# Queries of an attention block: transposed on TensorE, or loaded in 128-byte runs and turned on VectorE

## The chip, the cores and the metric

The kernel runs on one core of a Trainium2 chip. The metric is the time of one execution on the device in microseconds (us); shorter is better. TensorE multiplies matrices, VectorE and ScalarE work on elements, GpSimd reduces over partitions here, and SyncE (SP) issues all DMAs, in the order in which they are written.

## The reference

Attention over pooled keys and values, then a feed-forward layer with squared Relu. There are 8 batches of 576 tokens and 8 heads of 64; keys and values are averaged over groups of 8 tokens, so every token attends to 72 of them.

```python
k_p = k.reshape(B, H, Sp, pool, D).mean(axis=3)
v_p = v.reshape(B, H, Sp, pool, D).mean(axis=3)
scores = scale * np.matmul(q, k_p.transpose(0, 1, 3, 2))
scores = scores - np.max(scores, axis=-1, keepdims=True)
attn = np.exp(scores)
attn = attn / (np.sum(attn, axis=-1, keepdims=True) + 1e-09)
out = np.matmul(attn, v_p)                     # q, k, v: (8, 8, 576, 64) float32
x = out.transpose(0, 2, 1, 3).reshape(B * S, H * D)      # 4608 x 512
h = np.maximum(x @ w_in, 0.0)                  # w_in 512 x 2048
return h * h @ w_out                           # w_out 2048 x 512
```

## The kernel before

The 4608 tokens are cut into 12 chunks of 384 (`CH`). A chunk lies in one batch, or spans two (chunks 1, 4, 7 and 10); `segments` gives its parts. One step is one chunk and one block of 128 hidden columns, 16 steps a chunk. In step s the loop at the end (L691) issues `hidden` of step s on TensorE (12 products of 128x384: high and low parts of x and of the weights, three products for each of four blocks), then the TensorE parts of the attention work that is due in the step, `weigh_values` last, and then `project` of step s - 2 (nine products of 128x512). After them come the parts for the other engines, written in this order: the split of the hidden block of step s - 1 (`split_hidden`: gh on ScalarE, gl on VectorE), what follows the attention's matmuls (the functions that `transpose_q`, `scores` and `weigh_values` return), the stages that issue nothing on TensorE, the conversion of weights, the collected loads, and last Relu and square of step s (ScalarE, VectorE). Every engine keeps the order in which its instructions are written (`InOrder`).

Attention runs ahead of its chunk, one pair of heads after the other, four steps apart (`STEADY`: the first step of each pair, and the offset of each stage from it). A pair's query load is issued `QL` = 4 steps ahead of its first step (`load_q`: 96 partitions, runs of 1 KB or 512 bytes). Then follow `transpose_q` (offset 0: four transposes of 96x128 into PSUM; ScalarE copies the rows of each head from there as the high part, and VectorE subtracts it for the low part, which goes to the other 64 rows, so that a tile st has 128 rows with high and low part stacked), `scores` (1), `exponents` (3: VectorE subtracts the maximum, ScalarE makes exponents, GpSimd sums over the partitions into tot), `send_sums` (4), `fetch_sums` (5), `reciprocals` (6), `fetch_reciprocals` (7) and `weigh_values` (8: av on TensorE; VectorE multiplies by the fetched reciprocals into rb, ScalarE and VectorE split it into xh and xl). Stages 4 to 7 send a row through DRAM with small DMAs.

Tiles that matter here: q lies in a buffer that loads of keys and values share (`LD` = 4); st has one buffer (`STB`). Chunks 0 and 1 are handled in another way: in full precision, with tokens on the partitions.

Loads of keys and values and their pooling (`kv_steps`, VectorE's reductions kp and vp) are spread over the steps before a batch is needed.

Of the kernel before, what the change touches and what calls it, by code (L numbers as in the profile page):

```python
# [9 lines left out]
F32 = mybir.dt.float32  # L10
F32R = mybir.dt.float32r
# [3 lines left out]
ALU = mybir.AluOpType  # L15
# [22 lines left out]
def pooled_attn_relu2_ffn(  # L38
# [16 lines left out]
    PE, DVE, ACT, GP, SP = (InOrder(tc, e) for e in (nc.tensor, nc.vector, nc.scalar, nc.gpsimd, nc.sync))  # L55
    B, H, S, D = q.shape
# [3 lines left out]
    P = 128  # L60
    POOL = 8
    SP_ = S // POOL
# [3 lines left out]
    CH = 384  # L66
    QT = 96
# [4 lines left out]
    KR = KH * SP_  # L72
    KT = KR // QT
    SCALE = 1.0 / (D ** 0.5) / POOL
    LAG, QL = 2, 4

    IDLE = (10, 3)
    STB, SCB, LD, OB = 1, 2, 4, 3
# [5 lines left out]
    SPLIT = 6  # L84


    STEADY = ((-22, -18, -14, -10), (0, 1, 3, 4, 5, 6, 7, 8))
    KV0 = -35
    EARLY = ((-16, -13, -10, -7), (0, 1, 2, 3, 5))

# [6 lines left out]
    sb = ctx.enter_context(tc.tile_pool(name="sb", bufs=2))  # L97
# [21 lines left out]
    def load(dst, src):  # L119
        loads.append((dst, src))  # L120
# [14 lines left out]
    def w_tile(dt, name):  # L135
        return wts.tile([P, 2, 512], dt, name=name, tag="w", bufs=2 * NFC + 1)

    halves = {}

    def half_tile(kind, name):  # L140

        if kind not in halves:
            halves[kind] = w_tile(F32, name)
            return halves[kind][:, 0, :]
        return halves.pop(kind)[:, 1, :]
# [35 lines left out]
    kv, kf, loaded = {}, {}, {}  # L181
# [9 lines left out]
    def ld_tile(shape, name, early):  # L191

        if early:
            return half_tile("l", name)[:shape[0], :shape[1]]
        return sb.tile(shape, F32, name=name, tag="ld", bufs=LD)
# [93 lines left out]
    def segments(c):  # L289
        t, segs = c * CH, []  # L290
        while t < (c + 1) * CH:
            b = t // S
            n = min((b + 1) * S, (c + 1) * CH) - t
            segs.append((b, t - c * CH, n))
            t += n
        return segs

    def load_q(c, p):

        qt = loaded["q", c, p] = ld_tile([QT, 2 * CH // QT * D], f"q_{c}_{p}", c == 0).rearrange("s (h n) -> s h n", h=2)  # L300
        for b, o, n in segments(c):
            s0, g = c * CH + o - b * S, n // QT
            load(qt[:, :, o // QT * D:(o // QT + g) * D],
                 q[b, 2 * p:2 * p + 2, s0:s0 + n, :].rearrange("h (s g) d -> s h (g d)", g=g))

    xts = {}
    live = {}

    def transpose_q(c, p):


        pt = ps_a.tile([P, 512], F32, name=f"qps_{c}_{p}", tag="a")
        blocks = pt[:, :CH].rearrange("p (i t s) -> p i t s", i=2, s=QT)
        qt = loaded.pop(("q", c, p))
        for i in range(2):
            for t in range(NQ // 2):
                PE.transpose(blocks[:, i, t, :], qt[:, i, t * 2 * D:(t + 1) * 2 * D], ident[:QT, :QT])

        def then():
            if c < 2:  # L320
                st = live[c, p] = half_tile("s", f"st_{c}_{p}")[:, :CH]
                ACT.copy(st, pt[:, :CH])
                return
            st = live[c, p] = sb.tile([P, 2, CH], F32R, name=f"st_{c}_{p}", tag="st", bufs=STB)
            order = "p i (s t two) -> p i t s two" if len(segments(c)) == 1 else "p i (t s two) -> p i t s two"
            cols = st.rearrange(order, two=2, s=QT)
            halves = [(slice(i * D, (i + 1) * D), slice((1 - i) * D, (2 - i) * D), i) for i in range(2)]
            for own, oth, i in halves:
                ACT.copy(cols[own, :, :, :, i], blocks[own])
            for own, oth, i in halves:  # L330
                DVE.tensor_tensor(cols[oth, :, :, :, i], blocks[own], cols[own, :, :, :, i].bitcast(F32), op=ALU.subtract)

        return then

    def scores(c, p):

        st = live.pop((c, p))
        ss = [ps_a.tile([P, 512], F32, name=f"sps_{c}_{p}_{i}", tag="a") for i in range(2)]
        for i in range(2):
            h = 2 * p + i  # L340
            for b, o, n in segments(c):
                kh, kl, _ = kv[b]
                for j, kk in enumerate((kl, kh)):
                    PE.matmul(ss[i][:SP_, o:o + n], lhsT=kk[:, h * SP_:(h + 1) * SP_], rhs=st[:, i, o:o + n], start=j == 0, stop=j == 1)

        def then():
            sc = sb.tile([SP_, 2, CH], F32, name=f"sc_{c}_{p}", tag="sc", bufs=SCB)
            mx = reduced("mx", c, p)
            for i in range(2):
                ACT.copy(sc[:, i, :], ss[i][:SP_, :CH])  # L350
                GP.partition_all_reduce(mx[i], sc[:, i, :], channels=SP_, reduce_op=bass_isa.ReduceOp.max)
            live[c, p] = (sc, mx)

        return then

    def reduced(kind, c, p):
        return [sb.tile([SP_, CH], F32, name=f"{kind}_{c}_{p}_{i}", tag="mx", bufs=3) for i in range(2)]
# [210 lines left out]
    for i in range(NKT):  # L568
        load_k(0, i)
        if i % KT == KT - 1:  # L570
            load_q(0, i // KT)
    for p in range(2, NPAIR):
        load_q(0, p)
    for p in range(NPAIR):
        load_v_pair(0, p)
    for i in range(NKT):
        load_k(1, i)
    load_q(1, 0)

    need = {}  # L580
# [14 lines left out]
    for i in range(KT + 2):  # L595
        pool_k(0, i)
    transpose_k(0, 0)()
    transpose_q(0, 0)()
    transpose_q(0, 1)()
    pool_k(0, KT + 2)  # L600
    keep_busy(IDLE[1])
# [4 lines left out]
    for f in reversed(after):  # L606
        f()
    after = [pool_v_pair(0, 2), pool_v_pair(0, 3)]
    transpose_q(0, 2)()
    transpose_q(0, 3)()  # L610
    for f in after:
# [33 lines left out]
    t = 1e9  # L645
    for key in reversed(keys):
        t = min(t - 1 / RATE, need[key] - 1 - MARGIN)
# [22 lines left out]
            at(s + v_at[h] + 2, pool_v, b, h)  # L670

    ready = {0, 1}
    stages = (transpose_q, scores, exponents, send_sums, fetch_sums, reciprocals, fetch_reciprocals, weigh_values)
    for c in range(1, NCH):
        first, offsets = EARLY if c == 1 else STEADY
        names = (transpose_q, token_scores, token_normalise, token_turn, weigh_values) if c == 1 else stages
# [4 lines left out]
        for p in range(NPAIR):  # L681
            s = c * NFC + first[p]
# [5 lines left out]

    last = (to_float32, split_weights)
    on_pe = (transpose_k, transpose_q, scores, token_scores, token_turn, weigh_values)  # L690
    for s in range(-PRO, len(steps) + LAG):  # L691
        todo = work.get(s, [])
# [50 lines left out]
```

## Time and profile before

| | us |
|---|---|
| median of 3 runs | 961.65 (961.38 to 963.41) |
| the profiled execution: its span, first to last instruction | 959.9 |
| TensorE busy (matmuls) | 945.7, 99% |
| VectorE busy | 615.3, 64% |
| ScalarE busy | 451.5, 47% |
| GpSimd busy | 353.7, 37% |
| DMA: 51651 packets, 63.65 MB | 21% of 16 engines for the kernel's own queue |

The execution that the profiler took is described by its span alone; the time of a run also holds what lies around the span, 1.75 us against the median. Busy time of TensorE counts a matmul from its start to its modelled end, so neighbours overlap: what a matmul costs the queue is the distance from its start to the next one's. In a timeline, a number in brackets behind a row is idle time of the engine just before it and what ended it.

### The profile page before, as it was taken

The numbers are of one execution on the slowest core, as the hardware profiler recorded it, in microseconds if no ns is written. First come the engines' busy times: TensorE is split into PE (matmuls) and PEld (weight loads), VectorE is DVE, ScalarE is ACT, GpSimd is POOL, SyncE is SP. The second block draws the span as 40 slices with busy tenths as digits, with TensorE's granted clock in tenths as the row PEclk, the third lists the DMA queues.
The fourth block names the chain that finished last, engine by engine and source line by source line (L and its number), as shares of the span: only waits on it lengthen the run. The fifth ranks groups of instructions, "written<-read, shape, count | busy, mean of one in ns | idle before, by whom it ended". The sixth has DMA issues, their size and how long they took to land.

```text
span 959.9 us, 13537 instructions
## 1 busy us (share of the span) xinstructions
PE 945.7 (99%) x4972; PEld 805.7 (84%) x4972; DVE 615.3 (64%) x1028; ACT 451.5 (47%) x909; POOL 353.7 (37%) x215
## 2 busy tenths in 40 slices
PE   7899999999999999999999999999999999999998
PEld 6657678888888888888888888888888888888997
DVE  7989876667765556677865656766776565553221
ACT  3888766754434344444344344444444444432322
POOL 3900343534344343444353443434443434430000
PEclk9999999999999999999999999999999999999999
DMA  9973111022112112112112012112211210100000
GB/s 271 305 278 96 42 54 64 30 68 80 53 30 77 32 34 68 47 52 88 51 46 72 30 35 83 34 33 78 80 40 43 66 30 18 59 9 9 33 1 34
DMA packets 51651, 63.65 MB, mean 66 GB/s; under 512 B 13936, under 2 KB 32192, under 8 KB 51584
## 3 DMA queue, kind: packets, MB, share of 16 engines
q1 hardware_dynamic: 51584, 62.78, 21.0%
q8 instruction: 39, 0.64, 0.3%
q14 instruction: 28, 0.23, 0.1%
HBM read 53.08 MB, written 9.68 MB: 65 GB/s over the span
## 4 chain that ended last, share of the span: by engine, by line
PE 93%; DMA 4%; DVE 1%; ACT 1%; SPq 1%; issue 0%; DVEq 0%; ACTq 0%
PE o L34 43%; PE h L34 41%; PE av L34 4%; PE sps L34 3%; DMA q<-in_q_dram 2%; PE qps L34 1%; DMA v<-in_v_dram 1%; DMA k<-in_k_dram 1%; DVE wf_o L34 1%; DMA raw_o<-in_moe_w_out_dram 1%; SPq L34 1%; ACT te L34 0%; PE kps L34 0%; PE pps L34 0%; DVE tm L34 0%
## 5 line engine op out<-in xcount | busy, mean ns | idle before, releaser
L34 PE MATMUL h<-xh,w_i 128*128 128x384 f32 x1488 | 417.0, 341 | 0.0
L34 PE MATMUL o<-w_o,gh 128*128 128x512 f32 x1056 | 334.8, 398 | 0.0
L34 PEld LDWEIGHTS h<-xh,w_i 128*128 128x128 f32 x1488 | 272.8, 188 | 10.6 <-issue 2.2
L34 POOL PARTITION_ALL_REDUCE tot<-sc x80 | 201.5, 2566 | 205.9 <-issue 199.5
L34 PE MATMUL h<-xl,w_i 128*128 128x384 f32 x744 | 249.9, 336 | 0.0
L34 PEld LDWEIGHTS o<-w_o,gh 128*128 128x128 f32 x1056 | 192.5, 188 | 51.9 <-issue 16.5
L34 POOL PARTITION_ALL_REDUCE mx<-sc x80 | 119.5, 1541 | 284.6 <-ACT sc L34 284.6
L34 DVE TENSOR_TENSOR gl<-r,gh 128x384 fp32r<-128x384 f32 x176 | 143.5, 816 | 109.1 <-ACT gh L34 108.9
L34 PE MATMUL o<-w_o,gl 128*128 128x512 f32 x528 | 209.1, 396 | 0.0
L34 DVE TENSOR_TENSOR r<-r 128x384 f32<-128x384 f32 x160 | 105.6, 660 | 109.3 <-ACT r L34 108.9
L34 ACT CAST gh<-r 128x384 fp32r<-128x384 f32 x176 | 90.4, 514 | 149.7 <-DVE r L34 149.2
L34 PEld LDWEIGHTS h<-xl,w_i 128*128 128x128 f32 x744 | 139.7, 188 | 10.6 <-issue 3.1
L34 ACT ACTIVATE r<-h 128x384 f32<-128x384 f32 x192 | 94.2, 491 | 101.4 <-PE h L34 100.0
L34 PEld LDWEIGHTS o<-w_o,gl 128*128 128x128 f32 x528 | 99.1, 188 | 22.1
L34 DVE TENSOR_TENSOR st<-qps,st 64x384 fp32r<-64x384 f32 x80 | 60.7, 759 | 61.2 <-ACT st L34 60.3
L34 ACT CAST st<-qps 64x384 fp32r<-64x384 f32 x80 | 59.6, 745 | 58.9 <-PE qps L34 58.4
L34 ACT CAST xh<-rb 128x384 fp32r<-128x384 f32 x40 | 20.5, 513 | 94.6 <-DVE rb L34 94.6
L34 ACT ACTIVATE sc<-sc 72x384 f32<-72x384 f32 x80 | 39.7, 525 | 45.7 <-DVE sc L34 45.7
L34 DVE TENSOR_REDUCE vp<-v 72x64 f32<-72x512 f32 x48 | 50.9, 1061 | 0.0
L34 PE MATMUL av<-sc,vp 72*64 72x384 f32 (+1 forms) x256 | 43.6, 426 | 2.5 <-ACT sc L34 2.5
L34 PE MATMUL o<-wf_o,r 128*128 128x512 f32 x96 | 44.6, 600 | 0.0
L34 DVE TENSOR_REDUCE kp<-k 96x64 f32<-96x512 f32 x42 | 43.9, 1044 | 0.4 <-DMA k<-in_k_dram 0.2
(82 smaller groups left out, 708.7 us busy)
## 6 DMA issues: line engine op xcount, KB each, us to landing
k<-in_k_dram SPq DMA_DIRECT2D x48, 192.0 KB
out_dram<-ob SPq DMA_DIRECT2D x36, 256.0 KB
raw_i<-in_moe_w_in_dram SPq DMA_DIRECT2D x16, 512.0 KB
raw_o<-in_moe_w_out_dram SPq DMA_DIRECT2D x16, 512.0 KB
v<-in_v_dram SPq DMA_DIRECT2D x56, 144.0 KB
rb<-rd SPq DMA_DIRECT2D x80, 96.0 KB
q<-in_q_dram SPq DMA_DIRECT2D x30, 192.0 KB
q<-in_q_dram SPq DMA_DIRECT2D x32, 96.0 KB
```

The costliest lines, as they stand in the source:

```text
L34: return lambda *a, **k: self.tc.keep_in_program_order(f(*a, **k))
```

## The change

Chunks 0 and 1 stay as they are. From chunk 2 on a pair's queries are loaded in other pieces: a tile of 128 partitions by 384, and for each head and each half of its 64 columns one DMA which puts 32 tokens on 32 partitions, with 32 numbers of each, 128 bytes, side by side for every block of 32 tokens. `turn_q` turns the 32x32 blocks on VectorE, so that columns of the head lie on the partitions and tokens along the row, in their order. `split_q` makes the tile st from the turned tile, with the same two copies on ScalarE and two subtractions on VectorE. The matmuls of `scores` are the same, in another order. The loads are issued five steps ahead of the pair's first step, for chunk 1 too; the turn comes one step ahead of it, the split at offset 0. All later stages keep their steps.

```diff
-    LAG, QL = 2, 4
+    LAG, QL = 2, 5
-    STEADY = ((-22, -18, -14, -10), (0, 1, 3, 4, 5, 6, 7, 8))
+    STEADY = ((-22, -18, -14, -10), (-1, 0, 1, 3, 4, 5, 6, 7, 8))
     def load_q(c, p):
+        if c > 1:
+            qt = loaded["q", c, p] = ld_tile([P, CH], f"q_{c}_{p}", False)
+            for b, o, n in segments(c):
+                s0 = c * CH + o - b * S
+                for i in range(2):
+                    for half in range(2):
+                        r = i * D + half * 32
+                        load(qt[r:r + 32, o:o + n].rearrange("j (n e) -> j n e", e=32),
+                             q[b, 2 * p + i, s0:s0 + n, half * 32:half * 32 + 32].rearrange("(n j) e -> j n e", j=32))
+            return
...
         def then():                            # transpose_q
-            if c < 2:
-                st = live[c, p] = half_tile("s", f"st_{c}_{p}")[:, :CH]
-                ACT.copy(st, pt[:, :CH])
-                return
-            st = live[c, p] = sb.tile([P, 2, CH], F32R, name=f"st_{c}_{p}", tag="st", bufs=STB)
-            order = "p i (s t two) -> p i t s two" if len(segments(c)) == 1 else "p i (t s two) -> p i t s two"
-            cols = st.rearrange(order, two=2, s=QT)
-            halves = [(slice(i * D, (i + 1) * D), slice((1 - i) * D, (2 - i) * D), i) for i in range(2)]
-            for own, oth, i in halves:
-                ACT.copy(cols[own, :, :, :, i], blocks[own])
-            for own, oth, i in halves:
-                DVE.tensor_tensor(cols[oth, :, :, :, i], blocks[own], cols[own, :, :, :, i].bitcast(F32), op=ALU.subtract)
+            st = live[c, p] = half_tile("s", f"st_{c}_{p}")[:, :CH]
+            ACT.copy(st, pt[:, :CH])
...
+    def turn_q(c, p):
+        qt = loaded.pop(("q", c, p))
+        live[c, p] = sb.tile([P, CH], F32, name=f"qt_{c}_{p}", tag="qt", bufs=1)
+        DVE.transpose(live[c, p], qt)
+    def split_q(c, p):
+        qt = live[c, p]
+        st = live[c, p] = sb.tile([P, 2, CH], F32R, name=f"st_{c}_{p}", tag="st", bufs=STB)
+        halves = [(slice(i * D, (i + 1) * D), slice((1 - i) * D, (2 - i) * D), i) for i in range(2)]
+        for own, oth, i in halves:
+            ACT.copy(st[own, i, :], qt[own, :])
+        for own, oth, i in halves:
+            DVE.tensor_tensor(st[oth, i, :], qt[own, :], st[own, i, :].bitcast(F32), op=ALU.subtract)
...
     def scores(c, p):
-        for i in range(2):
-            h = 2 * p + i
-            for b, o, n in segments(c):
-                kh, kl, _ = kv[b]
+        for b, o, n in segments(c):
+            kh, kl, _ = kv[b]
+            for i in range(2):
+                h = 2 * p + i
                 for j, kk in enumerate((kl, kh)):
...
-    stages = (transpose_q, scores, exponents, send_sums, fetch_sums, reciprocals, fetch_reciprocals, weigh_values)
+    stages = (turn_q, split_q, scores, exponents, send_sums, fetch_sums, reciprocals, fetch_reciprocals, weigh_values)
```

## Rows read from the trace of the kernel before

**Rows 1.** The page: TensorE's busy time, and its granted clock in 40 slices.
```profile
PE 945.7 (99%) x4972; PEld 805.7 (84%) x4972; DVE 615.3 (64%) x1028; ACT 451.5 (47%) x909; POOL 353.7 (37%) x215
PEclk9999999999999999999999999999999999999999
```
**Rows 2.** The page: the chain that ended last, share of the span by engine.
```profile
PE 93%; DMA 4%; DVE 1%; ACT 1%; SPq 1%; issue 0%; DVEq 0%; ACTq 0%
```
**Rows 3.** Timeline of TensorE, 539.0 to 545: start, us, engine, operation, tiles, shape, count.
```profile
539.33 0.50 PE L34 MATMUL qps<-ident,q 96*128 96x96 f32 x4
539.75 0.87 PE L34 MATMUL av<-sc,vp 72*64 72x192 f32 x8
...
544.85 0.25 PE L34 MATMUL sps<-st,kl 128*72 128x192 f32 x1
```
**Rows 4.** Groups by shape, whole run: form, count, busy us, mean ns, idle before.
```profile
L34 DVE STREAM_TRANSPOSE ramp<-ramp 128x32 f32<-128x32 f32 x1 | 0.2, 211 | 0.0
...
L34 DVE TENSOR_SCALAR ramp<-ramp 128x1 f32<-128x1 f32 x1 | 0.2, 155 | 0.0
```
**Rows 5.** Timeline of VectorE, 532 to 551.
```profile
533.35 1.02 DVE L34 TENSOR_TENSOR sc<-sc,mx 72x384 f32<-72x384 f32 x2
535.92 0.77 DVE L34 TENSOR_TENSOR r<-r 128x384 f32<-128x384 f32 x1 [1.55 <-ACT r L34]
537.27 1.92 DVE L34 TENSOR_TENSOR gl<-r,gh 128x384 fp32r<-128x384 f32 x1 [0.58 <-ACT gh L34]
...
542.06 0.56 DVE L34 TENSOR_TENSOR rb<-av,rb 128x384 f32<-128x384 f32 x1
543.20 0.56 DVE L34 TENSOR_TENSOR xl<-rb,xh 128x384 fp32r<-128x384 f32 x1 [0.58 <-ACT xh L34]
...
549.58 0.16 DVE L34 TENSOR_SCALAR rr<-rc 96x8 f32<-96x8 f32 x1
```
**Rows 6.** Groups by shape in 325 to 400 (chunk 5, one batch).
```profile
L34 ACT CAST st<-qps 64x384 fp32r<-64x384 f32 x8 | 6.8, 851 | 7.7 <-PE qps L34 7.7
L34 DVE TENSOR_TENSOR st<-qps,st 64x384 fp32r<-64x384 f32 x8 | 6.8, 844 | 7.6 <-ACT st L34 7.6
```
**Rows 7.** Groups by shape in 250 to 325 (chunk 4, two batches).
```profile
L34 DVE TENSOR_TENSOR st<-qps,st 64x384 fp32r<-64x384 f32 x8 | 4.4, 556 | 5.2 <-ACT st L34 5.1
L34 ACT CAST st<-qps 64x384 fp32r<-64x384 f32 x8 | 4.0, 501 | 6.7 <-PE qps L34 6.7
```
**Rows 8.** Timeline of GpSimd, 534 to 541.
```profile
534.61 5.01 POOL L34 PARTITION_ALL_REDUCE tot<-sc  x2 [4.57 <-issue]
```
**Rows 9.** Timeline of VectorE, 481.5 to 490: the late pair.
```profile
483.58 1.92 DVE L34 TENSOR_TENSOR gl<-r,gh 128x384 fp32r<-128x384 f32 x1 [0.58 <-ACT gh L34]
```
**Rows 10.** Timeline of TensorE, 481.5 to 489.3: the late pair.
```profile
482.87 0.49 PE L34 MATMUL qps<-ident,q 96*128 96x96 f32 x4
483.30 0.87 PE L34 MATMUL av<-sc,vp 72*64 72x384 f32 x4
...
488.39 0.25 PE L34 MATMUL sps<-st,kl 128*72 128x192 f32 x1
```
**Rows 11.** The tile q: issues on SyncE, duration in ns min/median/max, first and last start.
```profile
L34 SPq DMA_DIRECT2D q<-in_q_dram x62: 325/346/810, 4.5 to 823.1; - x62
```
**Rows 12.** What SyncE's queue waited for: us in total, times, longest.
```profile
SPq L34 <- POOL tot L34: 200.4, 69, 22.0
```
**Rows 13.** DMA in 531.0 to 532.6: queue, packets, MB, share of 16 engines.
```profile
q1 hardware_dynamic: 112, 0.00, 3.6%
```
**Rows 14.** DMA in 521.4 to 524.
```profile
q1 hardware_dynamic: 580, 0.34, 48.6%
```
**Rows 15.** Timeline of SyncE's queue, 538 to 541.
```profile
540.80 0.32 SPq L34 DMA_DIRECT2D rc<-rs  x1
```
**Rows 16.** Timeline of TensorE, 102.4 to 112.5: waits at the start of chunk 2.
```profile
104.35 0.37 PE L34 MATMUL sps<-st,kl 128*72 128x384 f32 x1 [0.83 <-DVE st L34]
...
111.43 0.97 PE L34 MATMUL pps<-ident,te 96*72 96x96 f32 x8 [0.51 <-DVE te L34]
```

More of the change, by code (lines that the diff above doesn't have):

```diff
@@ L338, in scores @@
         ss = [ps_a.tile([P, 512], F32, name=f"sps_{c}_{p}_{i}", tag="a") for i in range(2)]
-        for i in range(2):
-            h = 2 * p + i
-            for b, o, n in segments(c):
-                kh, kl, _ = kv[b]
+        for b, o, n in segments(c):
+            kh, kl, _ = kv[b]
+            for i in range(2):
+                h = 2 * p + i
                 for j, kk in enumerate((kl, kh)):
-                    PE.matmul(ss[i][:SP_, o:o + n], lhsT=kk[:, h * SP_:(h + 1) * SP_], rhs=st[:, i, o:o + n], start=j == 0, stop=j == 1)
+                    PE.matmul(ss[i][:SP_, o:o + n], lhsT=kk[:, h * SP_:(h + 1) * SP_], rhs=st[:, i, o:o + n],
+                              start=j == 0, stop=j == 1)
         def then():
```

## The prediction

> **What bounds the kernel now.** I read the page first: matmuls fill 99% of the span, and the granted clock stays in its top tenth from end to end, so the clock is not where a change can act [rows 1]. The chain that ended last says the same from the other side: 93% of the end time hangs on TensorE's own work, one product behind the next, and the other engines hold it only near the start and the end [rows 2]. Then the timeline of TensorE for one pair of heads in the middle. The reader should look at starts, not at durations, since matmuls overlap: the four query transposes start at 539.33, the weighing of values behind them at 539.75, and nothing stands between [rows 3]. So whatever leaves TensorE's queue shortens the program by its start-to-start time, as long as the operands of the next products are there in time. The rest of the reading is about that condition.
>
> **What is removed.** From chunk 2 on (10 chunks of 4 pairs, 40 pairs), `transpose_q` no longer issues its four transposes: 160 matmuls go. One group of four costs 539.75 - 539.33 = 0.42 us of TensorE's queue, not four times a matmul's own duration; the late pair further on shows 0.43; I take 0.425. 40 x 0.425 = **17.0 us**. The products of `scores` keep their number and sizes; in chunks that span two batches only their order changes, which I cost at nothing. The bank of PSUM that the transposes used is freed.
>
> **What is added on VectorE.** `turn_q`, one transpose of 128x384 per pair, is nowhere in the trace at that size. Nearest rows: the 128x32 transpose took 211 ns, a 128x1 operation 155 ns [rows 4]. The 31 further columns cost 56 ns, 1.8 ns each, so 384 columns come to 155 + 383 x 1.8 = 0.85 us; at the rate of the other 128x384 operations it is 0.56 us [rows 5]. I take 0.7. It is queued one step ahead of the split, behind the two subtractions of `exponents`; there VectorE stands idle from 534.37 to 535.92, 1.55 us, while ScalarE makes exponents and the next Relu [rows 5]. The squaring of r is what waits behind it, and both ends fit into the gap. Without that cover it would delay the squaring by its own length, and behind that the products only where VectorE is already late (below).
>
> **What is moved.** The split of queries into high and low parts becomes `split_q`. It no longer reads PSUM nor writes every other or eighth column: in chunk 5, one batch, the strided forms take 851 ns on ScalarE and 844 ns on VectorE [rows 6]; in chunk 4, two batches, 501 and 556 ns [rows 7]. Contiguous tiles in SBUF should cost what chunk 4 shows: 0.50 and 0.56, four instructions per pair. For 28 of the 40 pairs that frees 0.7 us on ScalarE and 0.6 us on VectorE, which about pays for the turn.
>
> More important is the place. Now the split comes ahead of the work of `weigh_values`; afterwards it stands behind it in the same step, since `split_q` is not one of the stages that issue on TensorE. So it now waits for the weighing. From the start of rb to the start of xl is 543.20 - 542.06 = 1.14 us [rows 5]; then xl 0.56 and two subtractions of 0.56 (ScalarE's two casts, 1.0 us behind xh, run beside xl and the first of them): rb's start + 2.82. In the pair at 539.33 the weighing would start at 539.33 and end 0.87 later at 540.20, so the split ends at 543.02. Scores are due at 544.85 - 0.42 = 544.43 [rows 3]. **Margin 1.4 us.** With the long forms (0.85) the split ends 0.9 later and still fits.
>
> That margin is gone where VectorE comes late. Its subtraction gl took 1.92 us at 537.27 instead of 0.56 [rows 5], beside the two sums over partitions on GpSimd, 534.61 to 539.62 [rows 8]. In the pair at 482.87 the same gl starts only at 483.58 and ends at 485.50 [rows 9], because reductions of keys and values filled VectorE's steps before. Split's end: 485.50 + 2.82 = 488.32; scores due at 488.39 - 0.43 = 487.96 [rows 10]: TensorE would wait 0.36 us. Gl ends over 2 us behind the transposes' start in 10 of the 40 pairs. 10 x 0.36 = 3.6 us would be lost if each waited in full, but a wait lets VectorE catch up for the next pair, and the shorter split of one-batch chunks gives 0.5 us back in between. I take **-1.5 us**, bounds 0 and -5.
>
> The new subtractions read two SBUF tiles, as gl does, where the old ones read one. They can't meet the sums: they are queued behind gl, which has already waited them out [rows 5, 8]. The Trainium skill (SBUF — State Buffer, "Who interferes with whom") says that a VectorE instruction with two SBUF inputs contends with a GpSimd instruction that reads SBUF, and one with a single SBUF input outside the two-port modes does not. The trace agrees for gl (1.92 against 0.56). By that rule the turn, which has one input, would not be held by the sums, and the first half of the rival called late VectorE below would fall away; no run here shows a turn beside them yet.
>
> **Loads.** A query load becomes 4 DMAs (8 in two-batch chunks) of 128-byte runs, 1536 packets instead of 192 or 384, issued one step earlier, now behind the fetch of reciprocals and ahead of `send_sums`. SyncE: a query DMA takes 0.35 us to issue, 0.81 at most [rows 11]; 156 more in all, 54 us over 800, against 200 us that its queue waits for the sums alone [rows 12]. So the added 1.1 to 2.1 us a pair mostly fill a wait. Packets: 112 small ones took 3.6% of 16 engines for 1.6 us, 8.2 ns each [rows 13]; a mix with 512-byte and 2 KB runs 48.6% of 16 x 2.6 us over 580, 35 ns [rows 14]. A load is some 1600 packets with its semaphores, 100 an engine: 0.8 to 3.5 us, nearer to the first. It has four steps, some 19 us, to land. Behind it in the same queue go the sums and their fetch; the fetch is issued at 540.80 [rows 15] and used at 549.58 [rows 5], so with 2 us for landing about 6.5 us are spare. Cost: nothing, up to 1 us. The Trainium skill (DMA: Bandwidth & Descriptors, "Specifications") speaks against the change here: under 512 bytes a descriptor is read, modified and written, so line rate is lost. No row here shows a 128-byte run. At twice the price of the rows a load would take 1.6 to 7 us, still under the 12 us from which the third rival decides, so by the rule as by the rows the forecast stands; the rule speaks for that rival's side.
>
> The loads' buffers (4, shared with keys and values) are asked for in another order: some key and value loads now wait for the turn one step earlier than they waited for the transposes. They wait for one another already. Nothing added.
>
> **Start.** At chunk 2's first scores TensorE waits 0.83 us for the split, and 0.51 for the last turn of chunk 1 [rows 16]. ScalarE's two casts shrink there by 0.7 us, while the turn goes into a full VectorE. I take +0.6 us, bounds -0.5 and +1.3.
>
> **Sum.** 17.0 - 1.5 + 0.6 = 16.1 us. The profiled span is 959.9; the median of the runs, 961.65, is 1.75 above it. 959.9 - 16.1 = 943.8, plus 1.75: **945.5 us**.
>
> **The rivals.** *Late VectorE.* The stretches in which keys and values are reduced become bound by the chain of VectorE and ScalarE: the turn is held by the sums as gl is, the squaring slides between the two sums or behind the second, and gl ends up to 1.1 us later. Some 16 of 40 pairs (my estimate from VectorE's timeline: the ten late ones and their neighbours) then give nothing (16 x 0.425 = 6.8 lost), and the ten late ones wait 0.36 now and then: 17.0 - 6.8 - 3.6 = 6.6, or 955.0 at worst and about 950 half way. For it: r and gl are stretched just there [rows 5, 9]. Against: the turn reads one tile and starts before the sums do. Chance 0.2.
>
> *TensorE's time is not given back.* Then removing transposes would only lengthen waits: 961, within 0.2%. TensorE shows no idle time before the transposes or the weighing [rows 3], so 0.03.
>
> *Slow short runs, slower than before.* If a 128-byte packet holds an engine so long that sums and reciprocals, queued behind the load, come late for VectorE, every pair pays. The load is issued about 5.5 us ahead of the sums and 6.5 us are spare behind: it decides from 12 us a load, 120 ns a packet. At 150 ns it is 3 us late in 40 pairs: 959.9 + 120 - 16 + 1.75 = about 1066. Rows say 8 to 35 ns, so 0.04 with anything like it.
>
> **How the numbers follow.** The forecast has 0.73, the late VectorE 0.2, the others 0.03 and 0.04. The lower end: 17.0 + 1.3 without waits gives 943.3, rounded to 943.0. The upper end takes in the bounds of the waits (-5, -0.5, -1: 951.1) and the half-way rival: 951.5. About 0.2% is what a measurement of this kernel tells from no change; both first cases are faster by more: 0.93, same 0.03, slower 0.04.
>
> **What would show it.** Right: no qps from chunk 2 on; the weighing starts where the transposes did; st on both engines at 0.50 and 0.56; a turn of 0.56 to 0.85 us ahead of the squaring; short idle times of TensorE before sps in about ten pairs, released by VectorE. Wrong: idle before sps in most pairs, a turn stretched to 1.4 us or more, VectorE or SyncE waiting for query loads, packets of 128 bytes far above 35 ns, or a reciprocal that comes late.

## The result, and the profile after

| | before | after |
|---|---|---|
| median of 4 runs, us | 961.51 (961.34 to 963.41) | 950.57 (949.54 to 952.58) |
| ratio, 95% interval | | 0.988 [0.9862, 0.9898] |
| span of the profiled execution | 959.9 | 949.8 |
| first product of step 0 | 40.7 | 43.4 |
| from there to the end of TensorE's last product | 915.7 | 902.6 |

The kernel is faster by 10.9 us where the forecast had said 16.1; 950.57 lies in the forecast's range of 943.0 to 951.5, near its upper end. In the texts below, "step 0 to end" is the last row of the table: it ends with TensorE's last product, 3.5 to 3.8 us ahead of the end of the span. The page of the kernel after: busy times (instructions behind the x), granted clock of TensorE in 40 slices, DMA packets.

```profile
PE 936.4 (99%) x4812; PEld 791.7 (83%) x4812; DVE 621.1 (65%) x1068; ACT 432.5 (46%) x909; POOL 349.1 (37%) x215
...
PEclk9799999999999999999999999999999999999999
...
DMA packets 105604, 63.66 MB, mean 67 GB/s; under 512 B 77872, under 2 KB 86144, under 8 KB 105536
```

Against [rows 1], 160 matmuls are gone and TensorE still fills 99% of a shorter span. VectorE has 40 more instructions, ScalarE as many as before and less time in them. The packets have doubled. The second digit of the clock, 7, belongs to the late start of step 0 and comes up below.

The pair that [rows 3] shows, on TensorE (start, duration, tiles, shape, count): the product just ahead of the transposes before, then the same place after.

```profile
539.15 0.34 PE L34 MATMUL h<-xh,w_i 128*128 128x384 f32 x1
```
```profile
534.21 0.34 PE L34 MATMUL h<-xh,w_i 128*128 128x384 f32 x1
534.48 0.87 PE L34 MATMUL av<-sc,vp 72*64 72x192 f32 x8
535.28 0.73 PE L34 MATMUL o<-w_o,gh 128*128 128x512 f32 x2
535.85 0.39 PE L34 MATMUL o<-w_o,gl 128*128 128x512 f32 x1
```

No transposes stand ahead of the weighing. But read the starts: from the last hidden product to the first av there are 534.48 - 534.21 = 0.27 us, where one hidden product follows the other every 0.17. Before, the first transpose came 0.18 behind the hidden product, the other three followed every 0.08, and av came 0.17 behind the last: 539.75 - 539.15 = 0.60. So the distance has shrunk by 0.33 and not by 0.42, and the step to the weighing is about 0.09 us longer than the step to another hidden product or to a transpose, without any wait being named. This is where most of the missing gain went; the experiments take it up.

VectorE in the same step, to be held against [rows 5]:

```profile
528.41 1.01 DVE L34 TENSOR_TENSOR sc<-sc,mx 72x384 f32<-72x384 f32 x2
529.35 0.57 DVE L34 STREAM_TRANSPOSE qt<-q 128x384 f32<-128x384 f32 x1
530.98 0.77 DVE L34 TENSOR_TENSOR r<-r 128x384 f32<-128x384 f32 x1 [1.06 <-ACT r L34]
532.33 1.92 DVE L34 TENSOR_TENSOR gl<-r,gh 128x384 fp32r<-128x384 f32 x1 [0.58 <-ACT gh L34]
535.40 0.56 DVE L34 TENSOR_TENSOR rb<-av,rb 128x384 f32<-128x384 f32 x1 [1.16 <-PE av L34]
536.54 0.56 DVE L34 TENSOR_TENSOR xl<-rb,xh 128x384 fp32r<-128x384 f32 x1 [0.58 <-ACT xh L34]
537.13 1.14 DVE L34 TENSOR_TENSOR st<-qt,st 64x384 fp32r<-64x384 f32 x2
```

The turn stands where it was expected, in 0.57 us, and VectorE still idles 1.06 us ahead of the squaring. From rb's start to the end of the split there are 538.27 - 535.40 = 2.87 us (2.82 expected). Groups by shape over the whole run (count, busy, mean ns, idle before):

```profile
L34 DVE TENSOR_TENSOR st<-qt,st 64x384 fp32r<-64x384 f32 x80 | 44.2, 553 | 4.5 <-ACT st L34 2.0
...
L34 ACT CAST st<-qt 64x384 fp32r<-64x384 f32 x80 | 40.7, 509 | 1.0
...
L34 DVE STREAM_TRANSPOSE qt<-q 128x384 f32<-128x384 f32 x40 | 22.7, 568 | 0.0
```

In all chunks the split now costs what [rows 7] showed for two batches alone. The late pair of [rows 9, 10] is here, first on VectorE, then on TensorE:

```profile
479.42 1.92 DVE L34 TENSOR_TENSOR gl<-r,gh 128x384 fp32r<-128x384 f32 x1 [0.58 <-ACT gh L34]
...
482.98 1.14 DVE L34 TENSOR_TENSOR st<-qt,st 64x384 fp32r<-64x384 f32 x2
```
```profile
483.74 0.34 PE L34 MATMUL h<-xh,w_i 128*128 128x384 f32 x1
483.91 0.25 PE L34 MATMUL sps<-st,kl 128*72 128x192 f32 x1
484.00 0.25 PE L34 MATMUL sps<-st,kh 128*72 128x192 f32 x1
484.26 0.28 PE L34 MATMUL sps<-st,kl 128*72 128x192 f32 x1
...
484.82 0.66 PE L34 MATMUL o<-w_o,gh 128*128 128x512 f32 x2
485.31 0.39 PE L34 MATMUL o<-w_o,gl 128*128 128x512 f32 x1
```

The split ends at 484.12. The scores of the first head start at 483.91, when its half of the split is ready; those of the second head wait: 484.26 - 484.00 = 0.26 where 0.09 is the rule. So the late pair loses 0.17 us, not 0.36.

The loads: DMA in 530.9 to 532.2, where one load lands, and the wait of SyncE's queue that answers [rows 12].

```profile
q1 hardware_dynamic: 1209, 0.18, 78.0%
```
```profile
SPq L34 <- POOL tot L34: 116.2, 55, 19.6
```

0.78 x 16 x 1.3 us over 1209 packets are 13.4 ns a packet, between the 8.2 and 35 of [rows 13, 14]; 1191 of them are under 512 bytes. SyncE's longer issuing took 84 us of what it had waited for the sums; the prediction had 54, as it put a query DMA at 0.35 us, and the median is 0.44 here.

The start of chunk 2, as [rows 16]:

```profile
105.55 0.37 PE L34 MATMUL sps<-st,kl 128*72 128x384 f32 x1 [0.58 <-DVE st L34]
...
113.31 0.33 PE L34 MATMUL pps<-ident,te 96*72 96x96 f32 x2 [1.02 <-DVE te L34]
```

The first scores start after 0.25 us less of waiting, their second head waits 0.12 more, and the last turn of chunk 1 0.5 more.

The whole difference can be told from the distances between the starts of TensorE's instructions:

| from before to after, us | |
|---|---|
| 39 groups from the last hidden product over av to the next o: 1.40 to 1.07 each | -12.9 |
| the first pair's transposes, which stood ahead of no weighing | -0.3 |
| waits inside the scores (28.3 to 29.1 in all) | +0.8 |
| chunk 2's first scores | -0.2 |
| last turn of chunk 1 | +0.5 |
| a wait of a hidden product for ScalarE's r, 0.82 us ahead of 53.89 before, which is absent where step 0 starts late | -0.9 |
| step 0 to the end | -13.0 |
| step 0 starts later | +2.7 |
| small distances, what follows the last product | +0.2 |
| span | -10.1 |

Why step 0 starts later: core 0 in the window 20 to 32 us (busy time and count of PE, PEld, DVE, ACT, POOL; granted clock; DMA share; GB/s), after, then before.

```profile
20.00:32.00 12.00, 11.43 (x75) 8.85 (x73) 8.69 (x22) 7.70 (x17) 11.06 (x25) 0.57 0.98 311
```
```profile
20.00:32.00 12.00, 10.38 (x92) 7.69 (x92) 9.69 (x24) 10.11 (x21) 11.06 (x22) 1.00 0.96 304
```

TensorE was granted 0.57 on average, most of the window at the lower of its two levels (1.2 instead of 2.4 GHz), for 13.7 us in all; 75 matmuls fit in where 92 did. Up to step 0's first products, the lower level lasted 13.7 us in e0 and e1 too, 10.2 in f1, 3.4 in before, e2, e5 and e6, and did not occur in e3, e4, e7 and e8; the start of step 0 went with it: 42.4 to 43.5 where it was over 10 us, 40.0 to 40.7 elsewhere. Of these e2 to e8 all contain the change, so it belongs to an execution, not to the change. Whether the change makes it more frequent stays open: the mean granted clock was 0.995 or less in 5 of 10 executions of the kernel after and in 6 of 33 of before. To compare executions I use the time from step 0 to the end, and add the 0.9 us of the table where the start is late: 902.6 + 0.9 = 903.5 for the kernel after. By that measure the gain is 12.2 us. The wait near 53 us isn't equally long in all executions, so differences under 1 us need a count that begins behind it: from the 31st product of o, 81.2 us in before and 83.0 in after, to the last product there are 875.2 and 863.0 us, 12.2 less as well.

### The profile page after: what moved, and what is told of

Its sections match the earlier page's. It is cut to its first block, busy times and chain, and to the rows that moved or that the text cites. A ratio compares the mean times of both kernels' runs of the same rounds, so it can differ in the third digit from the quotient of the medians.

```text
span 949.8 us, 13475 instructions
## 1 busy us (share of the span) xinstructions
PE 936.4 (99%) x4812; PEld 791.7 (83%) x4812; DVE 621.1 (65%) x1068; ACT 432.5 (46%) x909; POOL 349.1 (37%) x215
## 4 chain that ended last, share of the span: by engine, by line
PE 91%; DVE 4%; ACT 3%; DMA 1%; issue 1%; SPq 0%; DVEq 0%; ACTq 0%
PE o L34 41%; PE h L34 40%; PE av L34 4%; PE sps L34 3%; DVE wf_o L34 1%; DVE wf_i L34 1%; ACT te L34 1%; PE idle L34 1%; DVE tm L34 1%; DMA vv<-in_v_dram 1%; PE pps L34 1%; PE vps L34 0%; DMA k<-in_k_dram 0%; DVE w_i L34 0%; ACT r L34 0%
## 5 line engine op out<-in xcount | busy, mean ns | idle before, releaser
L34 POOL PARTITION_ALL_REDUCE mx<-sc x80 | 116.8, 1507 | 268.4 <-ACT sc L34 268.4
L34 PEld LDWEIGHTS o<-w_o,gl 128*128 128x128 f32 x528 | 99.2, 188 | 22.2
L34 DVE TENSOR_TENSOR st<-qt,st 64x384 fp32r<-64x384 f32 x80 | 44.2, 553 | 4.5 <-ACT st L34 2.0
L34 ACT COPY sc<-sps 72x384 f32<-72x384 f32 x80 | 34.0, 475 | 23.6 <-PE sps L34 23.6
L34 DVE TENSOR_TENSOR rb<-av,rb 128x384 f32<-128x384 f32 x40 | 22.2, 554 | 33.6 <-PE av L34 33.3
```

Of the source, the lines that this page charges most:

```text
L34: return lambda *a, **k: self.tc.keep_in_program_order(f(*a, **k))
```

## The experiments

The theory (T): a change of TensorE from products with 128 columns of weights to av's 64 columns costs 0.09 us whatever stands ahead of it. Before, it lay between the last transpose and av and was counted into the group; as it stays, a group is worth 0.33 us and not 0.425. The rivals: the weighing now waits for an operand that comes late, TensorE waits for splits that come late (W), the turn is held by GpSimd's sums (S), the loads cost time (L). Each edit is to the kernel after unless it says otherwise.

**e0, the kernel after again.** No edit.

> The changed kernel itself, beside the others. The profile of it has 902.6 us from the first product of step 0 to the end (before: 915.7), but step 0 starts 2.7 us later, after a stretch of 10 us at the lower clock. If that late start is the clock's and differs from execution to execution, the start of step 0 here lies anywhere between 40.5 and 43.5 us while step 0 to end is 902.6 again within 0.3, and the median lies near 949.6 to 951.5. If the late start belongs to the changed kernel (its loads one step earlier), step 0 starts at 43.4 again whatever the clock.

Measured: 950.13 (948.65 to 954.38, 6 runs), ratio 0.9887 [0.9868, 0.9907]; from step 0 902.7. Step 0 starts at 43.5 again, so this run by itself leaves open whose the late start is; e2 to e8 settle it. Runs e0, e1, e2 and e8 shared a chip.

**e1, four transposes put back.** They turn a constant into a bank that nobody reads.

```diff
+        if c > 1:
+            idle = ps_a.tile([P, 512], F32, name=f"dum_{c}_{p}", tag="a")
+            for t in range(4):
+                PE.transpose(idle[:, t * QT:(t + 1) * QT], ident[:QT, :], ident[:QT, :QT])
         sc, rb = live.pop((c, p))          # weigh_values
```

> The changed kernel with four transposes of the identity put back ahead of each weighing, which nobody reads. Theory (a group of transposes is worth 4 x 0.083 = 0.33 us, since the 0.09 us between TensorE's full products and the first weighing product stay whatever stands ahead of it): plus 40 x 0.33 = 13.3 us over the changed kernel, step 0 to end 915.9, all of the gain given back and everything else in the change worth nothing. Rival (a group is worth the whole 0.425, and the changed kernel loses 0.09 elsewhere, because the weighing now waits for an operand): the four cover that wait too, the step behind is at 0.425 - 0.09 = 0.33 as well, so this run alone doesn't tell them apart; it tells whether the rest of the change costs anything: then the time lies above that of before.

Measured: 961.73, 1.0003 [0.9992, 1.0014] of the kernel before. The whole gain is gone: 915.2 from step 0, or 916.1 with the late start's 0.9, against 903.5: 12.6 us in 40 pairs, 0.32 each. From hidden product to av it is 0.60 again, 0.33 more than in the kernel after; 0.6 us come back because the second heads of the late pairs no longer wait. Four transposes are worth 0.33 us, put in as well as taken out. With them back, the time is 0.4 above that of before: whatever else the change moved (turn, split, loads) is worth little.

**e2, one transpose put back.** As e1, with range(1).

> The same with one transpose instead of four. Theory (change of tiling): one transpose costs its own 0.083, plus 40 x 0.083 = 3.3 us, step 0 to end 905.9; the distance from the last product ahead to the first weighing product is 0.17 + 0.17. Rival (the weighing waits 0.09 for an operand): the transpose of 0.083 fills that wait, plus 0 to 0.4 us, step 0 to end 902.6 to 903.0.

Measured: 953.53, 0.9915 [0.9900, 0.9931]; 906.5 from step 0, 3.0 above 903.5. TensorE in the pair shown above:

```profile
534.00 0.34 PE L34 MATMUL h<-xh,w_i 128*128 128x384 f32 x1
534.17 0.25 PE L34 MATMUL dum<-ident 96*128 96x96 f32 x1
534.35 0.87 PE L34 MATMUL av<-sc,vp 72*64 72x192 f32 x8
```

Hidden product to transpose 0.17, transpose to av 0.18: together 0.35, against 0.27 with nothing between them. One transpose costs 0.08, as much as the second to fourth of a group of four, and the 0.09 of the change remain whatever precedes. So a transpose there isn't hidden by the change, and the change has a price of its own.

**e8, the weighing in full width.** Weights of both heads side by side, 128 columns instead of 64; each head's half of the result is used.

```diff
+                    PE.matmul(wide[i][:, o:o + n],
+                              lhsT=kv[b][2][:, 2 * p:2 * p + 2, :].rearrange("s h d -> s (h d)"),
+                              rhs=sc[:, i, o:o + n], start=True, stop=True)
...
+                    DVE.tensor_tensor(rb[own], wide[i][own, :CH], rb[own], op=ALU.mult)
```

> The changed kernel with the weighing done at full width: each head's product takes the values of both heads as weights (72x128 instead of 72x64) and goes to a bank of its own, of which half is used; two multiplications of 64 rows take the place of one of 128. Theory (the 0.09 belong to the change between 128-column products and 64-column ones): the first weighing product starts 0.17 us behind the last hidden product instead of 0.27, and the products behind it start without the extra 0.09; as the two heads' products no longer run beside each other, a pair takes 4 x 0.32 + 0.17 = 1.46 instead of 1.06, plus 40 x 0.4 = 16 us. Rival (late operand): 0.27 stays.

Measured, one execution: 963.21; 917.2 from step 0, 13.7 above 903.5.

```profile
539.48 0.33 PE L34 MATMUL h<-xh,w_i 128*128 128x384 f32 x1
539.66 1.46 PE L34 MATMUL av<-sc,vp 72*128 72x192 f32 x8
540.82 0.77 PE L34 MATMUL o<-w_o,gh 128*128 128x512 f32 x2
541.43 0.39 PE L34 MATMUL o<-w_o,gl 128*128 128x512 f32 x1
```

The kernel is slower, since a group takes 1.16 us to o instead of 0.80; of the 13.7 us, 2.3 are new waits for and in the scores. What the run was for is the first distance: 539.66 - 539.48 = 0.18. With 128 columns the step is that of any other product, so the 0.09 come from the width. This agrees with the Trainium skill (TensorEngine Tiling (Array Packing), "Key Properties"), which says that a change of the tiling mode drains TensorE; it names no price.

Behind the group, distances between o products alone mislead: here the first o starts 0.03 us behind the last av, in the kernel after 0.26. So count from the first av to gl. Here it is 541.43 - 539.66 = 1.77 us, and eight products, one every 0.163, with two of o at 0.23 make 1.76: nothing is lost. In the kernel after it is 535.85 - 534.48 = 1.37, where four pairs of products, one pair every 0.163 as inside the long groups of e4, with the same two of o make 1.11: 0.26 too many. Where the 64-column products go, both losses go: 0.09 ahead and 0.26 from there on, 0.35 us a group. For the second part this may be the width, or that two narrow products run beside each other (they start 0.007 us apart), which this edit takes away too.

**e3, the split first.** `split_q` is issued ahead of what follows the weighing, which undoes the move within the step.

```diff
+        for f, a in todo:
+            if f is split_q:
+                f(*a)
         for f in later:
             f()
         for f, a in todo:
-            if f not in on_pe + last:
+            if f not in on_pe + last + (split_q,):
```

> The changed kernel with the split written ahead of what follows the weighing, as the splits of before were. Theory (place decides the margin, and the margin is missed in six or seven late pairs by 0.06 to 0.2 us and at chunk 2's start by 0.4): the split ends over 2 us ahead of the scores in ordinary pairs, the waits of 0.2 us inside the scores of the pairs at the start of chunks 4, 7 and 10 vanish, 0.6 us in all, and up to 0.4 at the start: step 0 to end 901.6 to 902.0. Rival (late VectorE binds the stretches in which keys and values are reduced): moving the split ahead would delay rb, xh and xl there by 1.1 us and change nothing in the waits: 902.6 or more.

Measured: 946.82, 0.9839 [0.9813, 0.9864]; 900.8 from step 0, 2.7 below 903.5: more than the 0.8 us of waits in the scores. VectorE at the late pair:

```profile
474.70 1.92 DVE L34 TENSOR_TENSOR gl<-r,gh 128x384 fp32r<-128x384 f32 x1 [0.58 <-ACT gh L34]
476.65 1.14 DVE L34 TENSOR_TENSOR st<-qt,st 64x384 fp32r<-64x384 f32 x2
477.82 0.56 DVE L34 TENSOR_TENSOR rb<-av,rb 128x384 f32<-128x384 f32 x1
```

The split follows gl at once and takes no time from rb that anyone misses. All waits in scores but 0.1 us at chunk 2's first are gone; the late pairs have 1.4 us to spare, others mostly 4.1. At the start of chunk 2 the first scores come 0.75 us earlier and the last turn of chunk 1 1.0, so W was real, and worth most at the start. e3 to e6 shared a chip.

**e4, e3 and the weighing of two pairs together.** The weighing of every even pair is put off by four steps, so that two follow each other; scores get a third buffer.

```diff
-    STB, SCB, LD, OB = 1, 2, 4, 3
+    STB, SCB, LD, OB = 1, 3, 4, 3
-                at(s + d, f, c, p)
+                at(s + d + (4 if f is weigh_values and c > 1 and p % 2 == 0 else 0), f, c, p)
```

> As the run with the split first, and the weighing of pairs 0 and 2 put off by four steps, so that two pairs are weighed in one step behind each other (one more buffer for their exponents). Theory (each change between full products and 64-column ones costs 0.09 us, in and out): 20 entries and 20 exits fewer, 40 x 0.09 = 3.7 us less than with the split first: step 0 to end 898 to 898.5, a median near 945.5. If the 0.09 belong to each weighing and not to the change of tiling, nothing is gained: 901.6 to 902. If VectorE comes late behind two weighings, TensorE waits before the scores of every second pair and a part is lost.

Measured: 939.18, 0.9758 [0.9734, 0.9782]: 22.2 us under the median of before beside it (961.42), better than both kernels. From step 0 893.6, 7.2 below e3. Twenty changes fewer in each direction, so a group costs 0.36 us beside its own products, twice what T had put down. On TensorE, a step whose weighing was put off, then one with two pairs:

```profile
520.58 0.62 PE L34 MATMUL o<-w_o,gh 128*128 128x512 f32 x2
521.04 0.40 PE L34 MATMUL o<-w_o,gl 128*128 128x512 f32 x1
...
524.60 0.34 PE L34 MATMUL h<-xh,w_i 128*128 128x384 f32 x1
524.86 1.52 PE L34 MATMUL av<-sc,vp 72*64 72x192 f32 x16
526.32 0.73 PE L34 MATMUL o<-w_o,gh 128*128 128x512 f32 x2
526.88 0.39 PE L34 MATMUL o<-w_o,gl 128*128 128x512 f32 x1
```

Sixteen products take 526.32 - 524.86 = 1.46 to o, two groups of eight 2 x 0.80: 0.14 less. With one step into the weighing saved that makes the 4.9 us (0.25 each) by which these groups shrink over the run. Another 2.5 us (0.12 each) come from the o products behind: the first two take 526.88 - 526.32 = 0.56 to gl here and 0.57 in the rows of after, but 521.04 - 520.58 = 0.46 where hidden products stand ahead, so each group less leaves a step of o quicker. 0.4 us are given back: the first pairs of chunks 4, 7 and 10 wait 0.14 each in their scores. By starts, the price of a group is 0.09 ahead of it, 0.15 in it (0.05 at its first pair of products, 0.10 between the last and o) and 0.11 in the first two of o. That this goes with the number of groups is shown here, that it goes with the narrow products by e8; why TensorE takes it is not shown.

**e5, the turn twice.**

```diff
         DVE.transpose(live[c, p], qt)
+        DVE.transpose(live[c, p], qt)
```

> The changed kernel with every turn done twice. Theory (the turn of 0.57 us stands in a gap of 1.5 us on VectorE): the second one fits too, ordinary pairs unchanged; only at chunk 2's start, where VectorE is full, up to 0.6 us: step 0 to end 902.6 to 903.3. Rival (late VectorE: the turn moves what is behind it in the late pairs): 10 pairs later by up to 0.57 each, 2 to 6 us more.

Measured: 951.22, 0.9878 [0.9851, 0.9904]; 903.6 from step 0, against 903.5; as the wait near 53 us was 0.6 shorter in this execution, the count from the 31st product of o is the one to read: 863.7, 0.7 above the 863.0 of after. VectorE, then GpSimd:

```profile
527.13 1.18 DVE L34 STREAM_TRANSPOSE qt<-q 128x384 f32<-128x384 f32 x2
528.77 0.77 DVE L34 TENSOR_TENSOR r<-r 128x384 f32<-128x384 f32 x1 [0.46 <-ACT r L34]
```
```profile
527.46 5.01 POOL L34 PARTITION_ALL_REDUCE tot<-sc  x2 [4.40 <-issue]
```

The second turn runs from 527.7 to 528.3 beside the first sum and takes 0.58; over all 80 the durations are 566 to 580 ns, the longer ones those of the second turns, which lie wholly beside a sum in 39 pairs. S falls. It agrees with the rule on one SBUF input that the prediction took from the Trainium skill (SBUF — State Buffer, "Who interferes with whom"). Even doubled, the turn costs only what it delays at chunk 2's first scores (0.6 us there).

**e6, each query load twice.** The second copy goes to a tile that nobody reads.

```diff
+                        if half == 0 and i == 0:
+                            q2 = sb.tile([P, CH], F32, name=f"q2_{c}_{p}_{b}", tag="ld2", bufs=2)
+                        load(q2[r:r + 32, o:o + n].rearrange("j (n e) -> j n e", e=32), ...)
```

> The changed kernel with every query load done twice, the second copy into a tile that nobody reads: 61440 more packets of 128 bytes and 208 more DMAs. Theory (a load is 1.2 us of the engines in 18.7 and its issue fills waits of SyncE's queue): no more than 0.5 us in all, step 0 to end 902.6 to 903.1. Rival (short runs cost time by coming ahead of the sums and the reciprocals): 1 us or more for each pair, 40 us.

Measured: 950.13, 0.9869 [0.9844, 0.9894]; 903.0 from step 0, and 863.1 from the 31st product of o against 863.0: no loss. SyncE's queue paid with its own waits, 116.2 in the kernel after:

```profile
SPq L34 <- POOL tot L34: 57.9, 23, 17.1
```

L falls.

**e7, scores in the order of before.** Head by head instead of batch by batch.

```diff
-        for b, o, n in segments(c):
-            kh, kl, _ = kv[b]
-            for i in range(2):
-                h = 2 * p + i
+        for i in range(2):
+            h = 2 * p + i
+            for b, o, n in segments(c):
+                kh, kl, _ = kv[b]
```

> The changed kernel with the order of the score products as before (all parts of one head, then the other). Theory (the first head's products start when the first half of the split is there and only the second head waits; in the late pairs of two-batch chunks the changed order brings the second head forward to the second segment's place): the waits of 0.2 us inside the scores of the first pairs of chunks 4, 7 and 10 shrink to under 0.05, 0.4 to 0.6 us less, step 0 to end 902.0 to 902.6 at a start of 43.4, up to 0.9 more with an earlier start. Rival (the matmuls wait for the whole split): they stay at 0.2.

Measured, one execution: 948.66; 902.9 from step 0, 0.6 below 903.5 (0.45 from the 31st product of o). The late pair:

```profile
481.39 0.25 PE L34 MATMUL sps<-st,kl 128*72 128x192 f32 x1
...
481.74 0.28 PE L34 MATMUL sps<-st,kl 128*72 128x192 f32 x1
481.85 0.25 PE L34 MATMUL sps<-st,kh 128*72 128x192 f32 x1
```

All four products of the first head run on the first half of the split, and the second head waits 0.02 us (0.11 between its first two products, where 0.09 is the rule) instead of 0.17. The scores of the whole run take 0.5 us less. So the new order, which the prediction costed at nothing, loses about half a microsecond by asking for the second half of the split earlier.

**f1, the kernel before with the weighing of two pairs together.** SCB = 3 and the same shift as in e4, on the kernel before.

> The kernel before, queries untouched, with the weighing of pairs 0 and 2 put off by four steps as in the run with two pairs. Theory (the change between full products and 64-column ones costs TensorE the same whatever stands ahead, so weighing in twos is worth what it was on top of the split first, 900.8 - 893.6 = 7.1 us for 20 changes): step 0 to end 908.5, a median near 954.4. Rival (most of the 7.1 came from waits of VectorE that only the changed kernel had): 912 or more.

Measured: 957.06, 0.9947 [0.9931, 0.9964]; 910.7 from step 0. Here step 0 begins while the clock is still at its lower level, which lasts to 44.67 us. Its first products in f1, then in before:

```profile
42.39 3.88 PE L34 MATMUL h<-x,wf_i 128*128 128x384 f32 x8
```
```profile
40.71 2.75 PE L34 MATMUL h<-x,wf_i 128*128 128x384 f32 x8
```

They take 1.1 us longer, which is the clock's and not the edit's: 910.7 - 1.1 + 0.9 for the late start makes 910.5. From the 31st product of o, behind all this, f1 is at 869.9, 5.2 us below before. So the price of a group is there without the change too, but less comes of it than the 7.1 expected: the groups and the o products behind them give 6.4 (7.4 in e4), and the hidden products' own distances 0.6, but 1.2 of that go to waits for and in the scores and 0.45 to the keys' transposes.

## Why the prediction was right and where it fell short

**The condition held.** What leaves TensorE's queue shortens the program: e1 takes the whole gain back by putting four products in. The rival that the time isn't given back is out.

**The price of a group was the step that failed.** 40 x 0.425 = 17.0 was mis-sized; the groups gave 13.2, or 0.33 each. The prediction read the distance from the first transpose to av, 0.42 [rows 3], as what goes away. What goes away is the distance from the product ahead of the transposes to av, less what the same step takes with nothing in between: the 0.09 by which the step into av is longer than the step into a transpose were in the 0.42, and they stay. The trace of before held that second number: chunk 11's last pairs are weighed when no queries are left to turn. Its TensorE there:

```profile
859.87 0.34 PE L34 MATMUL h<-xh,w_i 128*128 128x384 f32 x1
860.14 0.87 PE L34 MATMUL av<-sc,vp 72*64 72x384 f32 x4
```

0.27 us from hidden product to av, where with the transposes between them it is 0.60: 0.33. Forty times that is 13.2, what was measured, and 17.0 - 13.2 = 3.8 of the 4.0 us by which the sum was too high.

**The late pairs.** The place was right: in eight of the same ten pairs gl ends late, 2.4 to 2.5 us behind av's start, and the split ends 0.06 to 0.2 us behind the start of the scores. But only three of them wait, the first pairs of chunks 4, 7 and 10, 0.2 us each; with the second head of chunk 2's first scores it is 0.8 in all, where 1.5 was taken. The ordinary margin came out at 1.32 us (1.4 worked out). Two things made the waits short: the first head's products need only half of the split, and two of the ten pairs are no longer late. By e7, 0.5 of the 0.8 is owed to the new order of products, which the prediction had put at nothing.

**The start** was given as a gain of 0.6 within -0.5 and +1.3; it is a loss of 0.3 (0.2 gained at the first scores, 0.5 lost at chunk 1's last turn). Right was that a shorter split helps and a turn in a full VectorE hurts; the place of the split, which e3 shows to be worth 1.8 us just there, wasn't thought of.

So the terms are 13.2 - 0.8 - 0.3 = 12.1 instead of 17.0 - 1.5 + 0.6 = 16.1, and 12.2 is what the two profiles show from equal starts. The medians differ by 10.9; the rest is the later start of step 0 in some executions, which no term of the sum held: the two executions of after with a mean clock of 0.998 and 1.0 took 949.5 and 949.6, 11.9 to 12.0 below the median of before.

**VectorE late**, as the rival had it, did not come: the turn isn't held (e5), and r and gl are as long as before. The upper end of the range took the time in all the same, and that is luck: it was set by the bounds of the waits and half way to this rival, while the 17.0, the term that was wrong, had no bound of its own.

**The loads** cost nothing, as said, and still nothing when doubled. 128 bytes in 13.4 ns are 9.6 GB/s for an engine; the mixture of [rows 14], 586 bytes a packet, moved 16.7. By that the Trainium skill's remark on small descriptors (DMA: Bandwidth & Descriptors, "Specifications") is right on the rate; here there was time for it.

## What to carry to other kernels

To price an instruction that leaves a full TensorE, don't take the distance between its start and the next one's: look for a place in the same trace where its neighbours follow each other without it, and take the difference. Where narrow products stand between wide ones, count the groups: fewer, longer groups were worth more here (e4, 7 us) than the waits that the change itself brought. And of work that moves to another place in a step, ask which half of its result is needed first.

## What the runs showed that was not expected

- A step from products with 128 columns of weights into av's 64 costs 0.09 us, and such a group loses about 0.27 more from there on, partly in the first two wide products that follow: 0.36 us a group in e4, with no wait named in the trace, and nothing of it in e8, where av has 128 columns. One place with products of 64 rows shows the first part too in the kernel before (97.16 to 97.43, 0.27 from a hidden product to sps).
- VectorE turns 128x384 fp32 numbers in 568 ns, as long as its other operations of that shape, and beside GpSimd's sums too.
- The granted clock near 25 us differed between executions, whatever the kernel, and with it the start of step 0 by up to 3.5 us (40.0 to 43.5).
